# Diagonal blocks of a block-causal attention transposed from 64 partitions into 64 columns

## The chip, the cores and the metric

The kernel runs on one core of a Trainium2 chip. The metric is the device time of one execution in microseconds (us), the lower the better; the median of three executions of the kernel before is 1132.5 us (1131.85 to 1132.52).

## The reference, cut to what matters

Eight batches with eight heads each, 576 positions, head width 64. Attention is causal by blocks of 64 positions; its output, with the heads side by side (512 wide), goes through a low-rank mixing over positions (rank 32) and then a two-layer network (512 to 2048 to 512) with a residual.

```python
scores = scale * np.matmul(q, k.transpose(0, 1, 3, 2))
mask = block_i >= block_j                      # blocks of 64 positions
attn = np.exp(scores - np.max(scores, axis=-1, keepdims=True))
attn = attn / (np.sum(attn, axis=-1, keepdims=True) + 1e-09)
out = np.matmul(attn, v)
# x: out with the heads side by side
h = xt @ U @ V
u = x + h.transpose(0, 2, 1)
ch = np.maximum(u @ w_ch1, 0.0) @ w_ch2
return u + ch
```

## The kernel before, in words

**Order of the work.** Nothing is issued where it is written. Every step is a task of a planner (`Plan`): it has an engine, a cost in ns, a priority (the lower the earlier) and the tiles that it reads and writes. `Plan.issue` (L175) plays the tasks through with these costs and issues them in the order in which they would start. Each cost is shifted by up to 2% by a number that `VARIANT` (L61) sets, so another `VARIANT` gives another order. A task with `port=True`, and every task on GpSimd (POOL), takes a shared token, so that in the plan no VectorE (DVE) task of that kind runs beside one on POOL.

**Attention.** There are 64 heads. The 576 queries of a head are cut into five tiles: tile 0 holds queries 0 to 63, and tile i holds the 128 queries from 128 i - 64 on. Tile i has 128 i + 64 keys, so the tiles are 64, 192, 320, 448 and 576 keys wide. `softmax` (L1208) takes a group of tiles: TensorE (PE) writes the scores of the group into one PSUM bank, DVE takes the maximum of every row (L1255), ScalarE (ACT) takes the exponentials with their sums (L1266). An exponential waits for the maxima of all tiles of its group. Tile 4, the widest, has a PSUM tile of two banks (`bw`) of which there is one, and tile 1 stands beside it there; tiles 3 and 0 share a bank, tile 2 has its own. `normalise` takes the reciprocals on DVE (L1282, L1283) and multiplies the rows on POOL (L1292).

**Transposes.** `transpose` (L1304) turns the probabilities around, block by block of 128 keys, in four banks a head, with 15 transposes: a matmul with the block of probabilities as its weights and an identity matrix as the moving operand (L1325). Ten blocks have 128 queries that count. Five are the diagonal blocks, one for each tile, of which only 64 queries count. Before, these take 128 partitions and write 128 columns like the others: a permuted identity, `swap` (L1047), brings the 64 queries that count to the front, and the 64 columns behind them are written over by the next transposes, for which `moves` is sorted. ACT (L1302) and DVE (L1300 or L1344) copy the bank out, and `apply_v` (L1354) multiplies with V: heads 0 to 13 in float32 (L1368), the other 50 in two parts of reduced precision (L1384).

**What runs beside it.** From about 100 us on, the first part of the two-layer network runs in tasks of six float16 matmuls each with 288 moving columns (L661, L686) in two PSUM banks `bf`; their priority number is above that of all of attention, so they fill PE where attention has nothing ready. The rest of the network (`block_products`, L910) comes last. Weights are scaled to powers of two that `power` finds with two small matmuls (L418, weights of one column; L438, weights of one row), and `agree` (L491) makes two of these scales fit each other with eight tiny DVE instructions (L499 to L505).

Of the kernel before, what the change touches and what calls it, by code (L numbers as in the profile page):

```python
# [57 lines left out]
TAIL = {"PE": 165, "DVE": 78, "ACT": 105, "POOL": 20, "SP": 0}  # L58
INTO = {"PE": 355, "DVE": 60, "ACT": 60, "POOL": 200, "SP": 60}
NEAR, DL, PORT = 130, 3000, 200  # L60
VARIANT = 4  # L61
START = {"DVE": 5750, "ACT": 2750, "POOL": 3300, "SP": 700}
COL = 0.4555
LA, MP = 900.0, 500.0
# [214 lines left out]
def attention_then_mixer(  # L279
# [211 lines left out]
    def agree(prio):  # L491


        a, b, c, d = (scales[n] for n in range(4))

        def limits():
            t = joint.ap
            for x, y in ((0, 1), (1, 0)):
                nc.vector.scalar_tensor_tensor(out=t, in0=a[:, x : x + 1], scalar=0.125, in1=c[:, x : x + 1], op0=ALU.mult, op1=ALU.mult)  # L499
                nc.vector.scalar_tensor_tensor(out=t, in0=t, scalar=b[:, y : y + 1], in1=d[:, x : x + 1], op0=ALU.mult, op1=(ALU.min, ALU.max)[x])  # L500
                nc.vector.tensor_copy(d[:, x : x + 1], t)

        def ratio():
            nc.vector.scalar_tensor_tensor(out=joint.ap, in0=b[:, 0:1], scalar=2.0 ** -6, in1=d[:, 0:1], op0=ALU.mult, op1=ALU.mult)
            nc.vector.scalar_tensor_tensor(out=joint.ap, in0=joint.ap, scalar=a[:, 1:2], in1=c[:, 1:2], op0=ALU.mult, op1=ALU.mult)  # L505

        add("DVE", 1700, prio, limits, [a, b, c], [d, joint])
        add("DVE", 200, prio, ratio, [a, b, c, d], [joint])

    def level(w, bufs):  # L510

# [532 lines left out]
        factor[x] = buf(fp, [1, P], F32, f"factor{x}".replace(".", "_"))  # L1044
        nc.vector.memset(factor[x].ap, x)

    swap = buf(ap, [P, P], F32, "swap")  # L1047
    for a in (0, 64):
        nc.vector.tensor_copy(swap[:, a : a + 64], ident[:, 64 - a : P - a])
    warm = buf(ap, [P, 1], F32, "warm")  # L1050
    nc.vector.memset(warm.ap, 0.0)
    nc.scalar.activation(warm.ap, warm.ap, AF.Exp)
# [155 lines left out]
    def softmax(h, tiles, pr):  # L1208

        q1, k1, q2, k2, ss, mx = (r[h % len(r)] for r in (q1_r, k1_r, q2_r, k2_r, ss_r, mx_r))  # L1210
        raw = raw_r[h % len(raw_r)]
        wide = 4 in tiles
        bank = Buf(pool=banks_w if wide else banks_f if h < 8 and 3 in tiles else Rest(banks_a))

        parts, at = [], 0
        for i in tiles:
            parts.append((i, at))
            at += P * i + 64
        side = {1: (0, T), 0: (1, T), 2: (0, T)}

        def view(i, at):
            if i == 4:
                return bank[:, :, :T]
            rows, w = P if i else 64, P * i + 64
            return bank[:rows, side[i][0], side[i][1] : side[i][1] + w] if wide else bank[:rows, at : at + w]

        def products():
            for i, at in parts:
                qs = slice(P * i + 64 - (P if i else 64), P * i + 64)
                for j in range(2 if i == 4 else 1):  # L1230
                    o = bank[:, j, :T] if i == 4 else view(i, at)
                    ks = slice(j * T, j * T + T) if i == 4 else slice(0, P * i + 64)
                    if h < FS:
                        if not i:

                            o, qs = bank[:, 1, T : T + 64] if wide else bank[:, at : at + 64], slice(0, P)
                        nc.tensor.matmul(  # L1237
                            o, raw[:, qs], raw[:, S + ks.start : S + ks.stop], start=True, stop=True
                        )
                        continue  # L1240
                    nc.tensor.matmul(o, q1[:, qs], k1[:, ks], start=True, stop=False)
                    nc.tensor.matmul(o, q2[:, qs], k2[:, ks], start=False, stop=True)

        ns, ms = [], []
        for i in tiles:
            ns += [T] * 4 if i == 4 else [P * i + 64] * 2
            ms += [P if i else 64] * (4 if i == 4 else 2)
        if h < FS:
            add("PE", sum(1.667 * n for n in ns) / 2 + 60 * sum(i < 2 or i == 4 for i in tiles), pr, products, [raw], [bank])
        else:  # L1250
            add("PE", _pe(*ns, m=ms) + (60 if wide else 30 + 33 * sum(i < 2 for i in tiles)), pr, products, [q1, k1, q2, k2], [bank])
        for i, at in parts:
            add(
                "DVE", _dve(P * i + 64), pr,
                lambda i=i, at=at: nc.vector.tensor_reduce(  # L1255
                    out=mx[: P if i else 64, i : i + 1], in_=view(i, at), op=ALU.max, axis=AX.XY if i == 4 else AX.X,
                    negate=True,
                ),
                [bank], [mx.parts[i]],
            )  # L1260
        for i, at in parts:
            pt, rows = pt_r[i][h % PB[i]], P if i else 64

            def exponentials(i=i, at=at, pt=pt, rows=rows):
                out = pt[:rows, : P * i + 64]
                nc.scalar.activation(  # L1266
                    out.rearrange("p (j k) -> p j k", j=2) if i == 4 else out, view(i, at), AF.Exp,
                    bias=mx[:rows, i : i + 1], accum_out=ss[:rows, i, 0:1],
                )

            add(
                "ACT", _act(P * i + 64) + 188, pr, exponentials, [bank, *(mx.parts[i] for i in tiles)],
                [pt, ss.parts[i]],
            )

# [28 lines left out]
    def transpose(h, g, part, pr):  # L1304

        js = BLOCKS[g][part]
        bank, span = Buf(pool=banks_a), _span(g, js)
        n = span.stop - span.start


        moves = []
        for j in js:
            for i in range(5):
                q0 = max(P * i - 64, 0)
                a, b = max(q0, _first(g, j)), min(P * i + 64, QS[g + 1])
                if a < b:
                    c = _at(g, j).start - span.start + a - _first(g, j)
                    half = b - a < P
                    left = half and c + P > 512
                    moves.append((not half, i, j, swap if half and i and not left else ident, c - 64 if left else c))  # L1320
        moves.sort(key=lambda m: m[0])

        def products():
            for _, i, j, perm, a in moves:
                nc.tensor.transpose(  # L1325
                    out=bank[:, a : a + P], in_=pt_r[i][h % PB[i]][:, j * P : (j + 1) * P], identity=perm.ap
                )

        cost = 109 * len(moves)
        pts = [pt_r[i][h % PB[i]] for i in sorted({m[1] for m in moves})]  # L1330
        if h < FP:
            pw = pw_r[h % 2][g]
            b = pw.parts[part]
            add("PE", cost, pr, products, pts, [bank], hold=[b])
            copy((g, part) == (0, 1), n, pr, lambda: pw[:, span], lambda: bank[:, :n], [bank], [b])
            return
        ph, pl = ph_r[g], pl_r[g]
        bh, bl = ph.parts[part], pl.parts[part]
        add("PE", cost, pr, products, pts, [bank], hold=[bh, bl])
        copy(False, n, pr, lambda: ph[:, span], lambda: bank[:, :n], [bank], [bh])  # L1340
        m = n if js[-1] < 4 else n - 64
        low = slice(span.start, span.start + m)
        add(
            "DVE", _dve(m), pr, lambda: nc.vector.tensor_sub(pl[:, low], bank[:, :m], f32(ph[:, low])), [bank, bh], [bl]  # L1344
        )
        if m < n:

            end = _at(1, 4)
            add(
                "DVE", _dve(64) + 112, pr,  # L1350
                lambda: nc.vector.tensor_sub(ph[64:P, end], bank[0:64, m:n], f32(ph[0:64, end])), [bank, bh], [bh],
            )

    def apply_v(h, g, pr):  # L1354
# [6 lines left out]
        if h < FP:  # L1361
            vr, pt = vr_r[h // 2 % 2], pw_r[s][g]

            def whole_products():
                for j in range(NK[g]):

                    a, x = max(P * j - q0, 0), 5 * s + j
                    nc.tensor.matmul(  # L1368
                        bank[:, a:n], vr[:, x : x + 2, :], pt[:, _at(g, j)], start=(j == 0), stop=(j == NK[g] - 1)
                    )  # L1370

            cost = sum(5 + 1.667 * (n - max(P * j - q0, 0)) for j in range(NK[g]))
            add("PE", cost + 60, pr, whole_products, [vr, *pt.parts], [bank], hold=[xb])
            copy(False, n, pr, lambda: xt[me, q0:q1], lambda: bank[0:64, :n], [bank], [xb])
            return
        vs, tmp, ph, pl = vs_r[s], take(tmp_r, "tmp"), ph_r[g], pl_r[g]
# [107 lines left out]
    for h in range(NH):  # L1484
# [1 line left out]
        if h + 1 < NH:  # L1486
            split_qk(h + 1, max(pr - LA, 1.0))
        for g, tiles in ((1, (4, 3)), (0, (2, 1, 0))):
            for x in ((4, 1), (3, 0)) if g else ((2,),):
                softmax(h, x, pr + 10)  # L1490
            normalise(h, tiles, pr + 10)
        for g in (1, 0):
# [61 lines left out]
```

## Time and profile before

| | |
|---|---|
| median of 3 runs | 1132.5 us (1131.85 to 1132.52) |
| the profiled execution | 1132.52 us, its span 1130.7 us |
| PE busy | 1114.4 us, 99% of the span |
| DVE busy | 992.4 us, 88% |
| ACT busy | 809.8 us, 72% |
| POOL busy | 495.0 us, 44% |
| transposes of probabilities (L1325) | 960, of which 768 with `ident` and 192 with `swap` |

The profile is one execution. Matmuls overlap one another, and the end of a matmul is modelled, so the length of a single one says little; what one costs on PE is read from start to start. In a row of the timeline stand the start, the length from the first start to the last end, the engine and line, out<-in, the weights (rows\*columns), the moving operand (partitions x columns) and the count. `PE` is the matmul itself, `PEld` the load of its weights.

### The profile page before, as it was taken

Reading aid. Unit: us, or ns where it says so; the run is one execution under the profiler, and the core shown is the slowest. Engines: PE = TensorE matmul, PEld = TensorE weight load, DVE = VectorE, ACT = ScalarE, POOL = GpSimd, SP = SyncE. Lnnn points to the kernel's source line nnn. Section 1 sums busy time; section 2 is a strip of 40 time slices with the busy share of each in tenths; the row PEclk is TensorE's granted clock in tenths of the full one; section 3 lists DMA queues with packets and bytes.
Section 4 is the critical chain, followed back from the end, with each engine's and each line's share of the span. In section 5 each row is a group of like instructions: output and inputs, shape, how many; then the busy total and the mean of one; then the engine's idle time right before and its main releaser. Section 6 shows DMA issues by size and latency. Waiting matters only on the chain.

```text
span 1130.7 us, 25478 instructions
## 1 busy us (share of the span) xinstructions
PE 1114.4 (99%) x8952; PEld 929.1 (82%) x8952; DVE 992.4 (88%) x2247; ACT 809.8 (72%) x1994; POOL 495.0 (44%) x688
## 2 busy tenths in 40 slices
PE   9999999999999999999999999999999999999998
PEld 7787788888888888888888877777777777777776
DVE  6899899999889889899899765499999899998998
ACT  7878899999889889989998854254555555454543
POOL 5334558787787777787876676000000000000000
PEclk9999999999999999999999999999999999999999
DMA  4453656554563464545543141103122130404111
GB/s 127 129 148 117 181 153 173 145 158 128 145 164 104 137 176 129 149 149 138 148 122 88 55 148 58 59 22 105 54 74 76 52 116 12 127 12 116 33 53 43
DMA packets 76720, 122.14 MB, mean 108 GB/s; under 512 B 9008, under 2 KB 53040, under 8 KB 76592
## 3 DMA queue, kind: packets, MB, share of 16 engines
q1 hardware_dynamic: 76592, 120.51, 37.3%
q8 instruction: 71, 1.16, 0.4%
q14 instruction: 57, 0.47, 0.1%
HBM read 76.23 MB, written 29.49 MB: 94 GB/s over the span
## 4 chain that ended last, share of the span: by engine, by line
PE 67%; DVE 16%; ACT 10%; issue 3%; DMA 2%; POOL 1%; SPq 0%; ACTq 0%; DVEq 0%; POOLq 0%
PE bb L910 36%; PE bf L686 8%; PE bf L661 6%; PE ba L1325 5%; ACT p L1266 4%; DVE mx L1255 4%; DVE pl L1344 3%; PE ba L1384 3%; PE ba L1368 2%; ACT ph L1302 1%; DVE xt L1392 1%; PE bw L1237 1%; DMA raw<-in_qk_dram 1%; DVE hl L669 1%; DVE ut L1445 1%
## 5 line engine op out<-in xcount | busy, mean ns | idle before, releaser
L1292 POOL TENSOR_SCALAR p<-p,rv 128x576 f32<-128x576 f32 (+4 forms) x320 | 166.2, 533 | 88.1 <-DVE rv L1283 18.3
L910 PE MATMUL bb<-ph,w2l 128*128 128x288 f16 x560 | 151.0, 286 | 0.0
L910 PE MATMUL bb<-ph,w2h 128*128 128x288 f16 x560 | 151.0, 286 | 0.0
L910 PE MATMUL bb<-ph,w1h 128*128 128x288 f16 x560 | 148.7, 286 | 0.0
L910 PE MATMUL bb<-ph,w1l 128*128 128x288 f16 x560 | 148.7, 286 | 0.0
L832 ACT CAST ph<-hb 128x576 f16<-128x576 f32 x144 | 84.3, 590 | 82.8 <-PE bb L910 77.2
L910 PEld LDWEIGHTS <-w2h 128*128 128x128 f16 x1120 | 109.6, 98 | 27.5
L910 PEld LDWEIGHTS <-w1h 128*128 128x128 f16 x1120 | 109.6, 98 | 27.5
L1325 PE MATMUL ba<-ident,p 128*128 128x128 f32 x768 | 121.4, 275 | 2.7 <-POOL p L1292 1.5
L910 PE MATMUL bb<-pl,w2h 128*128 128x288 f16 x560 | 123.5, 286 | 0.0
L1344 DVE TENSOR_TENSOR pl<-ba,ph 128x512 fp32r<-128x512 f32 x200 | 105.8, 551 | 10.1 <-ACT ph L1302 7.1
L910 PE MATMUL bb<-pl,w1h 128*128 128x288 f16 x560 | 114.4, 286 | 0.0
L686 PE MATMUL bf<-hh,w2h 128*128 128x288 f16 x384 | 110.4, 287 | 0.2 <-DVE ot L698 0.2
L686 PE MATMUL bf<-hl,w2h 128*128 128x288 f16 x384 | 109.8, 286 | 0.0
L686 PE MATMUL bf<-hh,w2l 128*128 128x288 f16 x384 | 109.8, 286 | 0.0
L1325 PEld LDWEIGHTS ba<-ident,p 128*128 128x128 f32 x768 | 89.3, 141 | 9.4 <-issue 2.9
L1302 ACT CAST ph<-ba 128x512 fp32r<-128x512 f32 x200 | 92.0, 494 | 3.5 <-PE ba L1325 2.3
L834 DVE TENSOR_TENSOR pl<-hb,ph 128x576 f16<-128x576 f32 x144 | 91.4, 655 | 1.0
L686 PEld LDWEIGHTS <-w2h 128*128 128x128 f16 x768 | 75.1, 98 | 19.7 <-issue 1.1
L1266 ACT ACTIVATE p<-ba,mx 64x64 f32<-64x64 f32 (+1 forms) x176 | 86.0, 492 | 6.2 <-DVE mx L1255 5.4
L661 PEld LDWEIGHTS <-w1h 128*128 128x128 f16 x768 | 73.9, 98 | 18.7 <-issue 1.2
L1384 PE MATMUL ba<-ph,vs 128*128 128x256 f32 (+3 forms) x400 | 84.3, 269 | 0.5 <-DVE ut L1445 0.5
(191 smaller groups left out, 3105.4 us busy)
## 6 DMA issues: line engine op xcount, KB each, us to landing
raw<-in_qk_dram SPq DMA_DIRECT2D x63, 288.0 KB, 3.9
o_d<-ot SPq DMA_DIRECT2D x72, 144.0 KB, 1.8
vr<-in_v_dram SPq DMA_DIRECT2D x32, 320.0 KB, 3.6
ur<-u_d SPq DMA_DIRECT2D x64, 144.0 KB, 2.5
wr<-o_d SPq DMA_DIRECT2D x32, 288.0 KB, 3.1
out_dram<-wr SPq DMA_DIRECT2D x31, 288.0 KB, 2.3
st<-in_w_dram SPq DMA_DIRECT2D x16, 512.0 KB, 4.3
u_d<-ut SPq DMA_DIRECT2D x28, 288.0 KB, 2.5
```

The source lines that it names most:

```text
L661: nc.tensor.matmul(ps[:, :T], w()[wn][:, k, fs], m[k].ap, start=(i == 0), stop=(i == len(ops) - 1))
L686: nc.tensor.matmul(ps[:, :T], w()[wn][:, f, ms], hs[f][x].ap, start=(i == 0), stop=(i == len(ops) - 1))
L832: add("ACT", _act(n * T, True), E, lambda: nc.scalar.copy(h.ap[:, :n, :], x[0]()), [x[1]], [h])
L834: "DVE", _dve(n * T), E, lambda: nc.vector.tensor_sub(l.ap[:, :n, :], x[0](), h.ap[:, :n, :]), [x[1], h], [l],
L910: nc.tensor.matmul(bank[:, i, :T], x()[:, w(k)], p.ap[:, k, :], start=first and n == 0, stop=last and n == len(ops) - 1)
L1255: lambda i=i, at=at: nc.vector.tensor_reduce(out=mx[: P if i else 64, i : i + 1], in_=view(i, at), op=ALU.max, axis=AX.XY if i == 4 else AX.X,
L1266: nc.scalar.activation(out.rearrange("p (j k) -> p j k", j=2) if i == 4 else out, view(i, at), AF.Exp, bias=mx[:rows, i : i + 1], accum_ou ...
L1292: lambda x=x, rows=rows, i=i: nc.gpsimd.tensor_scalar(out=x, in0=x, scalar1=rv[:rows, i : i + 1], scalar2=1.0, op0=ALU.mult, op1=ALU.mult),
L1302: add("ACT", _act(n), pr, lambda: nc.scalar.copy(out(), inp()), reads, writes)
L1325: nc.tensor.transpose(out=bank[:, a : a + P], in_=pt_r[i][h % PB[i]][:, j * P : (j + 1) * P], identity=perm.ap)
L1344: "DVE", _dve(m), pr, lambda: nc.vector.tensor_sub(pl[:, low], bank[:, :m], f32(ph[:, low])), [bank, bh], [bl]
L1384: nc.tensor.matmul(bank[0 : c.stop, a:n], vs[:, j, c], x[:, _at(g, j)], start=(i == 0), stop=(i == len(ops) - 1))
```

## The change

Three things change in the work and some numbers in the planner.

1. A diagonal block is transposed from the 64 partitions that hold the queries that count (the first 64 for tile 0, the last 64 for the others), with the 64x64 corner of the identity as the moving operand, into 64 columns. `swap`, its two copies at the start and the sorting go; the moves of a bank stand in the order of keys and queries.
2. The groups of `softmax` are (4, 1, 0) and (3) in place of (4, 1) and (3, 0): tile 0 stands beside tiles 4 and 1 in the two-bank tile.
3. The tasks of `agree` take the token that keeps POOL away (`port=True`), with higher costs.
4. In the planner a 64-column transpose costs 55 instead of 109, the exponentials cost 6 more, the float32 product with V 30 more, and `VARIANT` is 210.

```diff
-VARIANT = 4
+VARIANT = 210
...
-        add("DVE", 1700, prio, limits, [a, b, c], [d, joint])
-        add("DVE", 200, prio, ratio, [a, b, c, d], [joint])
+        add("DVE", 2000, prio, limits, [a, b, c], [d, joint], port=True)
+        add("DVE", 450, prio, ratio, [a, b, c, d], [joint], port=True)
...
-    swap = buf(ap, [P, P], F32, "swap")
-    for a in (0, 64):
-        nc.vector.tensor_copy(swap[:, a : a + 64], ident[:, 64 - a : P - a])
...
-                "ACT", _act(P * i + 64) + 188, pr, exponentials, [bank, *(mx.parts[i] for i in tiles)],
+                "ACT", _act(P * i + 64) + 194, pr, exponentials, [bank, *(mx.parts[i] for i in tiles)],
...
                 if a < b:
-                    c = _at(g, j).start - span.start + a - _first(g, j)
-                    half = b - a < P
-                    left = half and c + P > 512
-                    moves.append((not half, i, j, swap if half and i and not left else ident, c - 64 if left else c))
-        moves.sort(key=lambda m: m[0])
+                    moves.append((i, j, _at(g, j).start - span.start + a - _first(g, j), b - a))
 
         def products():
-            for _, i, j, perm, a in moves:
+            for i, j, c, w in moves:
+                qs = slice(P - w, P) if i else slice(0, w)
                 nc.tensor.transpose(
-                    out=bank[:, a : a + P], in_=pt_r[i][h % PB[i]][:, j * P : (j + 1) * P], identity=perm.ap
+                    out=bank[:, c : c + w], in_=pt_r[i][h % PB[i]][qs, j * P : (j + 1) * P], identity=ident[qs, qs]
                 )
 
-        cost = 109 * len(moves)
+        cost = sum(109 if w == P else 55 for *_, w in moves)
...
-            add("PE", cost + 60, pr, whole_products, [vr, *pt.parts], [bank], hold=[xb])
+            add("PE", cost + 90, pr, whole_products, [vr, *pt.parts], [bank], hold=[xb])
...
-            for x in ((4, 1), (3, 0)) if g else ((2,),):
+            for x in ((4, 1, 0), (3,)) if g else ((2,),):
```

In the planned order of PE (engine queue, from its start; the names are out<-in, `ba` and `bf` PSUM banks, `p_0_n` the probabilities of a tile of head 0; the size is that of the output) the four banks of head 0 stand like this before:

```order
L1325 MATMUL ba_98<-swap,p_0_174 128x128
L1325 MATMUL ba_98<-ident,p_0_176 128x128
L1325 MATMUL ba_98<-ident,p_0_174 128x128
L1325 MATMUL ba_98<-ident,p_0_176 128x128 x2
L1325 MATMUL ba_95<-swap,p_0_170 128x128
L1325 MATMUL ba_95<-swap,p_0_172 128x128
L1325 MATMUL ba_95<-ident,p_0_172 128x128
L1325 MATMUL ba_96<-ident,p_0_168 128x128
L1325 MATMUL ba_96<-ident,p_0_170 128x128
L1325 MATMUL ba_96<-ident,p_0_172 128x128
```

and after, at the same place (L1320 is the same line of code):

```order
L1320 MATMUL ba_98<-ident,p_0_171 128x128
L1320 MATMUL ba_98<-ident,p_0_173 128x128
L1320 MATMUL ba_98<-ident,p_0_171 128x64
L1320 MATMUL ba_98<-ident,p_0_173 128x128
L1320 MATMUL ba_98<-ident,p_0_173 128x64
L1235 MATMUL bf_90<-raw_161 128x448
L1320 MATMUL ba_95<-ident,p_0_165 128x64
L1320 MATMUL ba_95<-ident,p_0_167 128x128
L1320 MATMUL ba_95<-ident,p_0_169 128x128
L1320 MATMUL ba_96<-ident,p_0_167 128x64
L1320 MATMUL ba_96<-ident,p_0_169 128x128
L1320 MATMUL ba_96<-ident,p_0_169 128x64
```

All ten rows before read 128 partitions; after, five of the eleven transposes read 64 partitions, and they alternate with those that read 128. Over the whole program 320 of the 960 transposes become ones of 64 partitions, and the order of PE changes 602 times between such a transpose and a matmul of another kind (301 times in, 301 times out).

The exponentials of head 0 on ACT before (`bw` is the two-bank tile, the names again out<-in):

```order
L1266 ACTIVATE p_0_176,ss_166<-bw,mx_189 128x576
L1266 ACTIVATE p_0_170,ss_166<-bw,mx_189 128x192
L1266 ACTIVATE p_0_174,ss_166<-bf_90,mx_189 128x448
L1266 ACTIVATE p_0_168,ss_166<-bf_90,mx_189 64x64
L1266 ACTIVATE p_0_172,ss_166<-ba_95,mx_189 128x320
```

and after:

```order
L1264 ACTIVATE p_0_173,ss_163<-bw,mx_186 128x576
L1264 ACTIVATE p_0_167,ss_163<-bw,mx_186 128x192
L1264 ACTIVATE p_0_165,ss_163<-bw,mx_186 64x64
L1264 ACTIVATE p_0_171,ss_163<-bf_90,mx_186 128x448
L1264 ACTIVATE p_0_169,ss_163<-ba_95,mx_186 128x320
```

The 64x64 tile has moved from the bank of tile 3 to the two-bank tile; the number of instructions is the same.

More of the change, by code (lines that the diff above doesn't have):

```diff
@@ L500, in limits @@
                 nc.vector.scalar_tensor_tensor(out=t, in0=t, scalar=b[:, y : y + 1], in1=d[:, x : x + 1], op0=ALU.mult, op1=(ALU.min, ALU.max)[x])
-                nc.vector.tensor_copy(d[:, x : x + 1], t)
+                last = nc.vector.tensor_copy(d[:, x : x + 1], t)
+            return last
         def ratio():
             nc.vector.scalar_tensor_tensor(out=joint.ap, in0=b[:, 0:1], scalar=2.0 ** -6, in1=d[:, 0:1], op0=ALU.mult, op1=ALU.mult)
-            nc.vector.scalar_tensor_tensor(out=joint.ap, in0=joint.ap, scalar=a[:, 1:2], in1=c[:, 1:2], op0=ALU.mult, op1=ALU.mult)
-        add("DVE", 1700, prio, limits, [a, b, c], [d, joint])
-        add("DVE", 200, prio, ratio, [a, b, c, d], [joint])
+            return nc.vector.scalar_tensor_tensor(out=joint.ap, in0=joint.ap, scalar=a[:, 1:2], in1=c[:, 1:2], op0=ALU.mult, op1=ALU.mult)
+        add("DVE", 2000, prio, limits, [a, b, c], [d, joint], port=True)
+        add("DVE", 450, prio, ratio, [a, b, c, d], [joint], port=True)
     def level(w, bufs):
@@ L1316, in transpose @@
                 if a < b:
-                    c = _at(g, j).start - span.start + a - _first(g, j)
-                    half = b - a < P
-                    left = half and c + P > 512
-                    moves.append((not half, i, j, swap if half and i and not left else ident, c - 64 if left else c))
-        moves.sort(key=lambda m: m[0])
+                    moves.append((i, j, _at(g, j).start - span.start + a - _first(g, j), b - a))
         def products():
-            for _, i, j, perm, a in moves:
+            for i, j, c, w in moves:
+                qs = slice(P - w, P) if i else slice(0, w)
                 nc.tensor.transpose(
-                    out=bank[:, a : a + P], in_=pt_r[i][h % PB[i]][:, j * P : (j + 1) * P], identity=perm.ap
+                    out=bank[:, c : c + w], in_=pt_r[i][h % PB[i]][qs, j * P : (j + 1) * P], identity=ident[qs, qs]
                 )
-        cost = 109 * len(moves)
-        pts = [pt_r[i][h % PB[i]] for i in sorted({m[1] for m in moves})]
+        cost = sum(109 if w == P else 55 for *_, w in moves)
+        pts = [pt_r[i][h % PB[i]] for i in sorted({m[0] for m in moves})]
         if h < FP:
```

## The prediction

> **What bounds the kernel now.** I read the page's totals first, then the busy time by stage, then the chain of work that ended last.
>
> ```profile
> span 1130.7 us, 25478 instructions
> ...
> PE 1114.4 (99%) x8952; PEld 929.1 (82%) x8952; DVE 992.4 (88%) x2247; ACT 809.8 (72%) x1994; POOL 495.0 (44%) x688
> ...
> PE 67%; DVE 16%; ACT 10%; issue 3%; DMA 2%; POOL 1%; SPq 0%; ACTq 0%; DVEq 0%; POOLq 0%
> ```
>
> PE is busy for 99% of the span, and two thirds of the chain run through it. The execution took 1132.52 us, 1.8 us more than its span, and it is the slowest of the three runs shown, 0.02 us above their median; so the sum below is made against 1132.5. Busy alone proves little, since matmuls overlap; the stages say more.
>
> ```profile
> core 0: us, PE busy (x) PEld busy (x) DVE busy (x) ACT busy (x) POOL busy (x), PEclk, DMA share, GB/s
> 0.00:100.00 100.00, 95.35 (x562) 78.96 (x563) 83.30 (x256) 78.87 (x226) 45.24 (x90) 1.00 0.47 133
> 133.00:141.00 8.00, 6.87 (x48) 5.94 (x46) 7.79 (x17) 6.34 (x15) 5.59 (x5) 1.00 0.85 221
> 200.00:600.00 400.00, 394.80 (x3336) 345.06 (x3334) 359.39 (x972) 364.04 (x1022) 314.49 (x440) 1.00 0.51 142
> 730.00:1130.00 400.00, 397.32 (x3244) 317.12 (x3241) 370.79 (x591) 200.51 (x339) 0.00 (x0) 1.00 0.21 63
> ```
>
> The clock is granted in full throughout (1.00). From 730 us on PE is a closed stream: 3244 matmuls in 400 us are 0.123 us each, and the rows of float16 matmuls below start 0.12 us apart. From 200 to 600 us attention and the first part of the network share PE, which stands idle for 5 us of 400, while DVE and ACT are at 90% and 91%. There is still network work left when attention is over:
>
> ```profile
> L686 PE MATMUL bf<-hh,w2h 128*128 128x288 f16 x102 | 29.2, 286 | 0.0
> ```
>
> This row (from the groups between 640 and 730 us) is one of six of its kind, 102 matmuls each of three and 96 each of three others. So a PE slot that attention gives back before 640 us can be filled with one of these 594 matmuls, and the end comes earlier by the same time. I take the sum of PE's work as what sets the end.
>
> **The transposes.** What one costs now, and what stands around it:
>
> ```profile
> 236.19 0.29 PE L686 MATMUL bf<-hl,w2h 128*128 128x288 f16 x1
> 236.32 0.60 PE L1325 MATMUL ba<-ident,p 128*128 128x128 f32 x4
> 236.75 0.27 PE L1325 MATMUL ba<-swap,p 128*128 128x128 f32 x1
> 236.86 0.93 PE L1325 MATMUL ba<-ident,p 128*128 128x128 f32 x7
> ```
>
> Four take 0.60 us with the last one 0.27 long, so they start (0.60 - 0.27)/3 = 0.11 us apart, and so does the one with `swap` (236.75 to 236.86). Is that the load of 128 columns of weights or the stream of 128 moving columns? Two places tell them apart. Half as many columns of weights:
>
> ```profile
> 369.64 0.29 PE L686 MATMUL bf<-hl,w2h 128*128 128x288 f16 x1
> 369.76 0.27 PE L1410 MATMUL ba<-ident,xt 128*64 128x128 f32 x1
> 369.87 0.29 PE L686 MATMUL bf<-hh,w2h 128*128 128x288 f16 x1
> ```
>
> A transpose with 64 columns of weights and 128 moving columns still holds PE for 0.11 us. And a transpose behind a short matmul:
>
> ```profile
> 606.99 0.40 PE L1425 MATMUL ba<-xl,ust 128*64 128x128 f32 x4
> 607.23 0.40 PE L1325 MATMUL ba<-ident,p 128*128 128x128 f32 x2
> ```
>
> The four of L1425 start (607.23 - 606.99)/4 = 0.06 us apart, and the transpose with its 128 columns of weights comes on at the same step: its load fits into 0.06 us. So the stream is the bound, at 0.109 us for 128 columns (0.60, 0.93 and 0.27 give 0.109 to 0.110). Float32 matmuls with other widths agree:
>
> ```profile
> 101.18 2.01 PE L1368 MATMUL ba<-spare,vr 128*128 128x256 f32 x10
> ```
>
> By L1368 these are six with 256 columns, two with 192 and two with 64; the first nine stream 1984 columns in 2.01 - 0.27 = 1.74 us, 0.88 ns a column, against 0.109/128 = 0.85 ns. A 64-column stream is then 0.055 us, just under the 0.06 that the load needs. I take 0.059 for a diagonal block, a saving of **0.050 us** each; the ends are 0.109 (the load counts after all: nothing saved) and 0.028 (if PE could step as for 64 columns of reduced precision, which I do not use since the load stands in its way).
>
> The Trainium skill speaks against the change here: "TensorE: Matmul & The Clock Gate", section on LDWEIGHTS, gives a load as the number of its columns over 1.2, 107 ns for 128, whatever the rows. By that alone the transposes would be bound by their loads and the sum would be zero; the trace differs, with 0.06 us.
>
> There are 320 diagonal blocks, five in each of 64 heads. The products with V (durations in ns, then first and last start in us) tell where the heads lie:
>
> ```profile
> L1368 PE MATMUL ba<-spare,vr x224: 219/352/537, 15.2 to 136.4; 128*128 128x256 f32 x42, 128*128 128x192 f32 x28, 128*128 128x64 f32 x28, 128*128 128x320 f32 x14
> L1384 PE MATMUL ba<-ph,vs x400: 191/267/416, 150.9 to 639.9; 128*128 128x256 f32 x51, 128*128 128x192 f32 x34, 128*128 128x64 f32 x33, 128*128 128x320 f32 x16
> ```
>
> Heads 14 to 63 take 489 us, some 10 us each, and run where the network fills PE: 250 x 0.050 = **12.5 us**. Heads 0 to 13 end at 136.4 us; before that PE is idle more (4.65 us of the first 100) and little else is ready; I count half of 70 x 0.050, **1.75 us** (ends 0 and 3.5).
>
> **The other edits.** `swap`'s copies are the first thing to go:
>
> ```profile
> 1.33 1.17 DVE L1049 COPY swap<-ident 128x64 f32<-128x64 f32 x2
> ...
> 6.90 1.02 DVE L1255 TENSOR_REDUCE mx<-bw 128x1 f32<-128x576 f32 x2 [3.05 <-PE bw L1237]
> ```
>
> DVE waits 3.05 us for the first scores afterwards, so this is worth nothing. Tile 0 beside tiles 4 and 1:
>
> ```profile
> L1255 DVE TENSOR_REDUCE mx<-ba 64x1 f32<-64x64 f32 x56 | 11.4, 204 | 0.2
> ...
> L1266 ACT ACTIVATE p<-ba,mx 64x64 f32<-64x64 f32 x56 | 17.4, 311 | 0.2
> ```
>
> The same instructions run; the exponentials of tile 4 wait for one more maximum (0.20 us), and the two-bank tile is held 0.20 + 0.31 us longer in a head of 10 us, while the bank of tile 3 comes free that much sooner. PE has network work under either wait: zero, and if that cover were gone, up to 0.2 us x 64 heads = 13 us against it at worst. `agree`:
>
> ```profile
> 133.68 0.54 DVE L499 SCALAR_TENSOR_TENSOR joint<-sc 128x1 f32<-128x1 f32 x1
> 134.26 0.79 DVE L500 SCALAR_TENSOR_TENSOR joint<-joint,sc 128x1 f32<-128x1 f32 x1
> ...
> 135.27 1.14 DVE L499 SCALAR_TENSOR_TENSOR joint<-sc 128x1 f32<-128x1 f32 x1
> 136.45 1.34 DVE L500 SCALAR_TENSOR_TENSOR joint<-joint,sc 128x1 f32<-128x1 f32 x1
> ...
> 138.82 0.15 DVE L504 SCALAR_TENSOR_TENSOR joint<-sc 128x1 f32<-128x1 f32 x1
> ```
>
> The four long ones take 3.81 us where one of that kind can take 0.15, so without POOL beside them up to 3.2 us go from DVE. Queued behind them are the maxima of the next head, and PE loses 8.00 - 6.87 = 1.13 us in this stretch. In return POOL's queue stands still for the planned 2000 + 450 ns. I count -0.5 us, with ends of -1.1 and +2.5. The new costs and `VARIANT` make the planner deal the same instructions in another order; no row prices that. The three runs lie 0.7 us apart, which is no measure of it; as an estimate I allow 4 us both ways, three quarters of PE's 5.2 idle us between 200 and 600.
>
> Sum: 12.5 + 1.75 + 0.5 = 14.75, and 1132.5 - 14.75 = **1118 us**. Own range of this case: 3.5 more or less for the first heads and `agree`, 4 for the order: 1111 to 1125.
>
> **The rivals.** *PE empties itself at every change of rows (slower).* There are places in the trace where PE stops between two matmuls that use different parts of its array:
>
> ```profile
> 500.86 0.29 PE L686 MATMUL bf<-hh,w2l 128*128 128x288 f16 x1
> 500.98 0.29 PE L686 MATMUL bf<-hl,w2h 128*128 128x288 f16 x1
> 501.20 0.38 PE L418 MATMUL ba<-ident,oneu 128*1 128x128 f32 x2
> 501.51 0.30 PE L686 MATMUL bf<-hh,w2h 128*128 128x288 f16 x1
> ...
> 260.00 0.38 PE L418 MATMUL ba<-ident,oneu 128*1 128x128 f32 x2
> 260.31 0.44 PE L1325 MATMUL ba<-ident,p 128*128 128x128 f32 x2
> ```
>
> Into L418 (weights of one column) the step is 0.22 instead of 0.12 us; its two matmuls step by 0.11, so they end at 501.42 and 260.22, and the next starts 0.09 later. A transpose behind it also shows its load (two take 0.44, not 0.38): 0.15 in all. If 64 rows beside 128 are such a change, it comes 602 times: 602 x 0.095 = 57 us, and 0.055 of load at the 301 changes into a diagonal block and at the 200 that lead to another transpose, 28 us. Less 16 saved that is 1132.5 + 69 = **1201 us** (without the loads 1173). It decides from 0.027 us a change on (16/602). Against it: weights of 64 columns beside 128 show no stop at all (369.76 to 369.87 and 607.23 above). No row here has 64 rows. The Trainium skill, "TensorEngine Tiling (Array Packing)", Key Properties, says that changing the tiling mode drains TensorE; the trace agrees for one column, and not for 64 columns. I give it 0.20.
>
> *The load is not hidden.* If the load is the floor (0.11 us whatever the moving columns), or a load for 64 rows can't run under a matmul of 128, each diagonal block gives back what it saved: 1132.5 us; if it is laid bare on the way out too, 602 x 0.055 - 16 = 17 us more, **1132 to 1150**. For it: the load behind L418 is shown in full. Against it: 607.23. 0.06.
>
> *Attention is paced by DVE and ACT.* At 90% and 91% they may be what the heads wait for; then PE's freed slots help only as far as the network's own steps on DVE and ACT find room, and I count a quarter of the gain: **1129 us**. Against it: PE idles 5 us in 400. 0.06.
>
> **How the numbers follow.** Forecast 0.68, the stops 0.20, the load 0.06, DVE and ACT 0.06. The likeliest is the first: 1118 us. The range leaves out the stops alone, on top of a tenth of the first case on its low side: 1109 to 1150. A measurement can tell some 0.2% (2.3 us) from no change. Faster: 0.68 + 0.05; within 0.2%: 0.02 of the load and 0.01 of DVE and ACT, with 0.01 for a bad order; slower: 0.20 + 0.03.
>
> **What would show it.** Right: 320 transposes of 64 rows that start about 0.06 us apart from what follows; first part of the network done some 13 us earlier, the last stage as long as before. Wrong: 0.2 us and more from a 128-row transpose to a 64-row one, and a weight load that starts about 0.09 us behind the end of the stream. PE's idle time between 200 and 600 us well over 5 us would mean that other engines pace the heads.

## The result and the profile after

The changed kernel takes **1180.89 us** (median of 4 runs, 1180.61 to 1181.47), the kernel before beside it 1132.51 us (4 runs): a ratio of 1.0427, with a 95% interval of 1.0409 to 1.0445. It is slower by 48.4 us, where 1118 was forecast and 1150 was the upper end of the range. The first rival, stops at changes of rows, comes nearest, with 1201 us (1173 without its loads).

From the page of the kernel after: the span, the totals of the engines and the shares of the chain that ended last.

```profile
span 1179.7 us, 25430 instructions
...
PE 1169.6 (99%) x8952; PEld 933.7 (79%) x8952; DVE 994.2 (84%) x2245; ACT 825.3 (70%) x1994; POOL 494.8 (42%) x688
...
PE 94%; ACT 3%; DVE 1%; DMA 1%; issue 1%; POOL 0%; SPq 0%; ACTq 0%
```

PE has the same 8952 matmuls and is busy for 55.2 us more (1169.6 against 1114.4); the record of a matmul lasts some 0.27 us, so a stop that is shorter counts as busy. Its idle time falls from 1130.7 - 1114.4 = 16.3 us to 10.1, so the span grows by 49.0. The chain, two thirds PE before, is now PE nearly alone; DVE's 16% and ACT's 10% in it have gone to 1% and 3%.

Busy time by stage of the kernel after; the last row is the last stage, taken from 780 us on, where 730 was taken before.

```profile
core 0: us, PE busy (x) PEld busy (x) DVE busy (x) ACT busy (x) POOL busy (x), PEclk, DMA share, GB/s
0.00:100.00 100.00, 96.77 (x518) 73.62 (x519) 72.67 (x225) 75.10 (x210) 43.26 (x84) 1.00 0.41 119
133.00:141.00 8.00, 8.00 (x65) 6.68 (x64) 6.28 (x18) 7.64 (x22) 4.95 (x10) 1.00 0.56 136
200.00:600.00 400.00, 399.32 (x3102) 322.97 (x3100) 335.78 (x896) 342.18 (x934) 289.65 (x406) 1.00 0.48 133
780.00:1180.00 400.00, 396.28 (x3235) 316.23 (x3233) 369.60 (x589) 199.89 (x338) 0.00 (x0) 1.00 0.22 63
```

From 200 to 600 us PE is busy for 399.32 us and does 3102 matmuls, where it did 3336 with 5 us idle. Each now takes more of PE's time, at a clock that is still granted in full; DVE, ACT and POOL all do less in the same stretch, so they wait for PE. The last stage is what it was (3235 matmuls in 400 us, before 3244).

The weight loads of one bank in the kernel after (timeline in several narrow windows, starting just before the sixth of six 128-row transposes; start and length in us):

```profile
527.00 0.15 PEld L1320 LDWEIGHTS ba<-ident,p 128*128 128x128 f32 x1
527.30 0.14 PEld L1320 LDWEIGHTS ba<-ident,p 64*128 64x128 f32 x1 [0.16 <-issue]
527.51 0.14 PEld L1320 LDWEIGHTS ba<-ident,p 128*128 128x128 f32 x1
527.77 0.14 PEld L1320 LDWEIGHTS ba<-ident,p 64*128 64x128 f32 x1
527.97 0.10 PEld L687 LDWEIGHTS <-w2h 128*128 128x128 f16 x1
```

And the matmuls that belong to the first four of these loads, at the end of one row of nine:

```profile
526.44 0.29 PE L687 MATMUL bf<-hl,w2h 128*128 128x288 f16 x1
526.56 1.48 PE L1320 MATMUL ba<-ident,p 128*128 128x128 f32 x9
527.97 0.30 PE L687 MATMUL bf<-hh,w2h 128*128 128x288 f16 x1
```

The row of nine is six 128-row transposes, then 64, 128 and 64 rows. At 0.109 us each the sixth starts at 526.56 + 5 x 0.109 = 527.10 and its stream ends at 527.21. The load of the first 64-row one starts only at 527.30: PE stands for **0.09 us**, and nothing is waited for that the profile names ("issue"). From the 64-row one to the next it is 0.21 us: its load, no longer hidden (0.055), its stream (0.055) and a second stop. The 128-row one between takes 0.26: its load laid bare, 0.109, and again a stop. The three take 527.97 - 527.21 = 0.76 us where three 128-row transposes took 0.33, so each diagonal block costs 0.22 us more than it did. Many such blocks show in the groups by shape of the kernel after, where loads of 64 rows have 19.1 us of "issue" ahead of them, which is not named at its loads of 128 rows:

```profile
L1320 PEld LDWEIGHTS ba<-ident,p 128*128 128x128 f32 x640 | 75.1, 141 | 17.2 <-POOL p L1290 1.6 <-ACT p L1264 0.2 <-POOL z L379 0.2
L1320 PEld LDWEIGHTS ba<-ident,p 64*128 64x128 f32 x320 | 40.8, 135 | 45.3 <-issue 19.1 <-POOL p L1290 1.5 <-DVE pl L1339 1.2
```

Where in the program the time came in, by the first and last products with V and of the network's first part, after:

```profile
L1379 PE MATMUL ba<-ph,vs x400: 191/266/415, 155.9 to 700.4; 128*128 128x256 f32 x51, 128*128 128x192 f32 x34, 128*128 128x64 f32 x33, 128*128 128x320 f32 x16
L687 PE MATMUL bf<-hh,w2h x384: 282/286/301, 136.5 to 773.7; 128*128 128x288 f16 x192
```

and of the network's first part before (the products with V stand in the prediction):

```profile
L686 PE MATMUL bf<-hh,w2h x384: 283/286/302, 122.4 to 722.5; 128*128 128x288 f16 x192
```

The first 14 heads are 5.0 us later (150.9 to 155.9), the other 50 take 544.5 us in place of 489.0, and 9 us come back after attention: 73.3 us of network are left then, before 82.6, since more of it was done beside attention. The last stage begins some 51 us late.

### The profile page after: what moved, and what is told of

Same layout as the page of the kernel before. It is cut to its first block, busy times and chain, and to the rows that moved or that the text cites. A ratio compares the mean times of both kernels' runs of the same rounds, so it can differ in the third digit from the quotient of the medians.

```text
span 1179.7 us, 25430 instructions
## 1 busy us (share of the span) xinstructions
PE 1169.6 (99%) x8952; PEld 933.7 (79%) x8952; DVE 994.2 (84%) x2245; ACT 825.3 (70%) x1994; POOL 494.8 (42%) x688
## 4 chain that ended last, share of the span: by engine, by line
PE 94%; ACT 3%; DVE 1%; DMA 1%; issue 1%; POOL 0%; SPq 0%; ACTq 0%
PE bb L911 35%; PE ba L1320 13%; PE bf L687 12%; PE bf L662 11%; PE ba L1379 6%; PE ba L1363 3%; PE bw L1239 2%; PE bw L1235 2%; PE bw L1240 2%; PE ba L1405 1%; PE ba L1420 1%; PE ba L1239 1%; PE ba L1240 1%; PE ba L1235 1%; ACT p L1264 1%; PE ba L1435 1%
## 5 line engine op out<-in xcount | busy, mean ns | idle before, releaser
L1320 PE MATMUL ba<-ident,p 128*128 128x128 f32 (+1 forms) x960 | 182.1, 284 | 1.3 <-POOL p L1290 1.3
L1320 PEld LDWEIGHTS ba<-ident,p 128*128 128x128 f32 (+1 forms) x960 | 115.9, 139 | 62.5 <-issue 19.4
L1300 ACT CAST ph<-ba 128x512 fp32r<-128x512 f32 x200 | 95.4, 492 | 27.1 <-PE ba L1320 23.7
L1264 ACT ACTIVATE p<-bw,mx 128x576 f32<-128x576 f32 (+2 forms) x192 | 92.9, 488 | 4.9 <-DVE mx L1253 3.9
L1253 DVE TENSOR_REDUCE mx<-bw 128x1 f32<-128x576 f32 (+2 forms) x192 | 77.8, 431 | 9.3 <-PE bw L1235 7.7
```

The costliest lines, as they stand in the source:

```text
L1253: lambda i=i, at=at: nc.vector.tensor_reduce(out=mx[: P if i else 64, i : i + 1], in_=view(i, at), op=ALU.max, axis=AX.XY if i == 4 else AX.X,
L1264: nc.scalar.activation(out.rearrange("p (j k) -> p j k", j=2) if i == 4 else out, view(i, at), AF.Exp, bias=mx[:rows, i : i + 1], accum_ou ...
L1300: add("ACT", _act(n), pr, lambda: nc.scalar.copy(out(), inp()), reads, writes)
L1320: nc.tensor.transpose(out=bank[:, c : c + w], in_=pt_r[i][h % PB[i]][qs, j * P : (j + 1) * P], identity=ident[qs, qs])
```

## The experiments

The theories: **stops** (PE empties at each change between 64 and 128 rows, the first rival); **load** (a load for 64 rows is not hidden, and no more); **order** (it is the planner's new order, or another of the edits, and not the transposes). The eight kernels ran on two chips, four on each; the kernel before took 1132.16 us (13 runs) and 1132.23 us (7 runs) there.

**One part alone, and the rest alone.** The kernel before with nothing but the 64-row transposes and their cost in the planner (in part; `swap` and the sorting go as in the change):

```diff
 # to the kernel before
...
+                qs = slice(P - w, P) if i else slice(0, w)
-                    out=bank[:, a : a + P], in_=pt_r[i][h % PB[i]][:, j * P : (j + 1) * P], identity=perm.ap
+                    out=bank[:, c : c + w], in_=pt_r[i][h % PB[i]][qs, j * P : (j + 1) * P], identity=ident[qs, qs]
...
-        cost = 109 * len(moves)
+        cost = sum(109 if w == P else 55 for *_, w in moves)
```

> The kernel before with the 64-row transposes alone; grouping, agree, planner numbers and VARIANT stay as before. Theory A (PE empties itself at each of some 600 changes between 64-row and 128-row matmuls, 0.09 us and an uncovered load): the whole slowdown is here, 1175 to 1200 us, and a 128-row transpose ahead of a 64-row one takes about 0.20 us instead of 0.11. Theory B (the other edits, above all tile 0 beside the widest tile, and the new order cost the time): 1118 to 1136 us.

Measured: 1189.59 us, ratio 1.0509 (1.0493 to 1.0524).

The changed kernel with the transposes of before (`swap`, 128 rows, the sorting), so with the grouping, `agree`, the other costs and `VARIANT` 210 (in part):

```diff
 # to the kernel after
...
-                qs = slice(P - w, P) if i else slice(0, w)
-                    out=bank[:, c : c + w], in_=pt_r[i][h % PB[i]][qs, j * P : (j + 1) * P], identity=ident[qs, qs]
+                    out=bank[:, a : a + P], in_=pt_r[i][h % PB[i]][:, j * P : (j + 1) * P], identity=perm.ap
```

> The changed kernel with the transposes of before (128 rows, 128 columns, the permuted identity); all its other edits stay. Theory A: 1132 us give or take 5, since the other edits move no PE work. Theory B: 1175 us or more.

Measured: 1132.81 us, ratio 1.0007 (0.9998 to 1.0017, 10 runs). The chains of the two, 64-row transposes alone first:

```profile
PE 90%; DVE 5%; ACT 3%; issue 1%; DMA 1%; SPq 0%; POOL 0%; ACTq 0%; DVEq 0%
```

```profile
PE 73%; DVE 12%; ACT 11%; issue 3%; POOL 1%; DMA 0%; SPq 0%; ACTq 0%; POOLq 0%
```

The transposes alone bring all of the loss, and the move of the chain to PE with it; on the kernel before the rest is neutral. Order falls as the cause. Together the two do not simply add up: beside the 64-row transposes the rest saves 8.7 us (1189.59 against 1180.89). From 700 to 800 us PE is idle for 5.6 us with the transposes alone and for none in the changed kernel; which of the other edits does that, no run shows.

**64 columns without 64 rows.** Each diagonal transpose is replaced by a float16 matmul of zeros with 128 rows and 64 moving columns, in the changed kernel and in the one with the 64-row transposes alone (the edit in part). The diagonal blocks are left out of the result by this.

```diff
+    blank = buf(ap, [P, P], F16, "blank")
+    nc.vector.memset(blank.ap, 0.0)
...
+                if w < P:
+                    nc.tensor.matmul(bank[:, c : c + w], blank.ap, blank[:, 0:w], start=True, stop=True)
+                    continue
```

> The changed kernel with the same float16 matmuls of zeros in place of the diagonal transposes (the diagonal blocks are left out of the product with V). Theory A: about 1113 us, as with the rest of before, 65 us below the changed kernel. Theory B: not below 1160 us, since tile 0 still stands beside the widest tile.

Measured: 1117.33 us (1115.12 to 1119.04), ratio 0.9868 (0.9854 to 0.9883).

> As the 64-row transposes alone, but in place of each diagonal transpose stands a float16 matmul of zeros with 128 rows and 64 moving columns into the same place; the diagonal blocks of the probabilities are left out of the product with V. The work per diagonal block falls from 0.109 to about 0.05 us on PE and no change of rows is left. Theory A, and the sum of PE's work sets the end: 320 x 0.06 = 19 us less than before, about 1113 us. If DVE and ACT pace the heads instead: 1126 us or more. Theory B has nothing to say of it.

Measured: 1126.93 us, ratio 0.9954 (0.9937 to 0.9971). That is not the 1113 us of the theory that PE's sum sets the end, but what was expected if DVE and ACT pace the heads.

The matmuls of a bank in the first of the two (timeline of PE):

```profile
285.56 0.20 PE L1323 MATMUL ba<-blank 128*128 128x64 f16 x1
285.60 0.31 PE L1325 MATMUL ba<-ident,p 128*128 128x128 f32 x1
285.74 0.19 PE L1323 MATMUL ba<-blank 128*128 128x64 f16 x1
285.77 0.41 PE L662 MATMUL bf<-uh,w1l 128*128 128x288 f16 x2
```

With 128 rows there is no stop on either side: 0.03 us to the next matmul (285.74 to 285.77). The transpose behind the first one takes 0.14 us in place of 0.109, as part of its load shows. The three take 285.77 - 285.56 = 0.21 us where three 128-column transposes took 0.33, so a block costs some 0.06 us less, 19 us for 320 of them (an estimate from this bank), and 14.8 us come through (1132.16 - 1117.33). So a saving on PE's path is worth most of its size in this kernel, as the forecast had assumed; that it is the rows that spoil it, the next run shows. With the order and the other edits of before, the same cut brought only 5.2 us. In that kernel PE is idle for 6.9 us in one stretch of a hundred, and the granted clock is 0.98 there:

```profile
600.00:700.00 100.00, 93.09 (x760) 74.15 (x759) 69.91 (x151) 64.64 (x135) 57.85 (x63) 0.98 0.27 84
```

The kernel before has 0.95 us of idle time and a clock of 1.00 in the same stretch, the end of attention. The longest waits of PE there are for steps of the network itself, 2.8 us for ACT (L644) and 2.8 us for DVE (L669). So a cut on PE is worth its size only where the network's own steps keep up.

**64 rows without float32 and without transposing.** The same matmul of zeros, now from 64 rows (the diagonal blocks are left out again):

```diff
 # to the kernel with the float16 matmuls and all other edits
-                    nc.tensor.matmul(bank[:, c : c + w], blank.ap, blank[:, 0:w], start=True, stop=True)
+                    nc.tensor.matmul(bank[:, c : c + w], blank[qs, :], blank[qs, 0:w], start=True, stop=True)
```

> The changed kernel with float16 matmuls of zeros in place of the diagonal transposes, as in the run at 1117 us, but with 64 rows in place of 128 (the diagonal blocks are left out of the product with V). If any change of rows stops PE: 602 x 0.09 us more, 1165 to 1180 us. If only transposes, or only float32, do: 1112 to 1122 us.

Measured: 1160.00 us, ratio 1.0247 (1.0232 to 1.0262), a little below the 1165 to 1180 expected if any change of rows stops PE. A bank of it, on the timelines of PE and of its loads:

```profile
284.84 0.27 PE L1410 MATMUL ba<-ident,xt 128*128 128x128 f32 x1
285.04 0.09 PEld L1323 LDWEIGHTS <-blank 64*128 64x128 f16 x1 [0.17 <-issue]
285.05 0.20 PE L1323 MATMUL ba<-blank 64*128 64x64 f16 x1
285.18 0.33 PE L1325 MATMUL ba<-ident,p 128*128 128x128 f32 x1
285.44 0.20 PE L1323 MATMUL ba<-blank 64*128 64x64 f16 x1
285.57 0.30 PE L687 MATMUL bf<-hh,w2h 128*128 128x288 f16 x1
```

Rows are the only difference to the kernel of 1117.33 us, and they cost 42.7 us, 0.071 for each of 602 changes (less than a stop: from the one kernel to the other PE's waits fall from some 42 us to 23, by the estimate explained with the rival's size below). The transpose of L1410 streams until 284.84 + 0.109 = 284.95, and the load of the 64-row matmul starts 0.09 us later. The step out of a 64-row matmul is 0.13 us where it was 0.03, so PE stops for 0.09 to 0.10 us on that side too; the 128-row transpose takes 0.26, with its float32 load laid bare. Neither the number format nor the transposing makes the stop. Load alone falls with this: the load itself starts late, and with float16 the loss stays.

**Fewer changes.** The 64-row transposes of a bank first, so that some stand side by side: 384 changes of rows in place of 602.

```diff
 # to the kernel after, ahead of products()
+        moves.sort(key=lambda m: m[3])
```

> The changed kernel with the 64-row transposes of a bank put ahead of its 128-row ones: the same 960 transposes, but 384 changes of rows in place of 602. If the cost hangs on the changes (0.09 us each over some 1125 us without any): about 1160 us, and two 64-row transposes in a row start some 0.06 us apart. If a 64-row transpose is slow by itself, wherever it stands: 1180 us as before, and 0.2 us between the two.

Measured: 1152.25 us, ratio 1.0179 (1.0162 to 1.0196), where about 1160 was expected if the cost hangs on the changes. Two 64-row loads on the same rows side by side in it, and the 128-row one behind them (timeline in several narrow windows; the second row counts the second load and the third together, the last row is the third alone):

```profile
438.53 0.13 PEld L1322 LDWEIGHTS ba<-ident,p 64*128 64x128 f32 x1 [0.17 <-ACT p L1264]
...
438.58 0.34 PEld L1322 LDWEIGHTS ba<-ident,p 64*128 64x128 f32 x2
438.79 0.14 PEld L1322 LDWEIGHTS ba<-ident,p 128*128 128x128 f32 x1
```

The same 960 transposes with 218 changes fewer are 28.6 us faster, 0.131 us a change, which lies between a stop alone (0.09) and a stop with a bare load (0.15). In between the two 64-row loads, some 0.055 us apart, there is no stop; behind the second there is one (0.34 - 0.14 = 0.20 us from load to load). As matmuls the two start 0.11 us apart (so do most of the 128 such pairs), the bare load of the first and its stream, and not 0.20; so a 64-row transpose is not slow by itself.

**Which rows.** All 64-row transposes read partitions 0 to 63 in place of 64 to 127 for tiles 1 to 4; their diagonal blocks are left out of the result by this.

```diff
 # to the kernel after
-                qs = slice(P - w, P) if i else slice(0, w)
+                qs = slice(0, w)
```

> The changed kernel with every 64-row transpose taken from partitions 0 to 63 in place of 64 to 127 (for tiles 1 to 4 the masked rows, so their diagonal blocks are left out). If the number of rows makes the stop: 1176 to 1186 us. If it is the start at partition 64: most stops go, 1125 to 1140 us.

Measured: 1182.31 us, ratio 1.0443 (1.0427 to 1.0458). It does not matter whether the 64 rows are the first or the last.

**The order alone.** The kernel before with `VARIANT` 210:

```diff
-VARIANT = 4
+VARIANT = 210
```

> The kernel before with VARIANT = 210 alone: the same instructions in another order. It measures what an order is worth: 1128 to 1137 us if my allowance of 4 us holds; more than that would put part of the 48 us on the order.

Measured: 1139.44 us (1137.79 to 1141.42), ratio 1.0066 (1.0051 to 1.0081). The same instructions dealt in another order cost 7.2 us, while with the other edits this number makes nothing slower (1.0007 above). A part of it goes with the clock: three of the four executions were granted 0.997 or 0.998 of it, and the one at 1.000 took 1137.79 us, 5.6 more than before.

None of these versions that computes the whole result is faster than the kernel before. A transpose from 128 rows into 64 columns, for which the float16 matmuls of 128 rows stand, was not tried.

## Why the prediction was wrong

- **PE's sum sets the end**: right for the changed kernel, where 55.2 us more of busy PE and 6.2 us less idle are the 49.0 of the span. For a saving it depends on the order: without 64 rows a cut of some 19 us brought 14.8 with the new order and the other edits, and 5.2 without them.
- **A 64-column stream takes 0.055 to 0.059 us**: right, where nothing changes around it (438.53 to 438.58). The saving of 0.050 a block would be there, but every 64-row block in these runs has a change of rows beside it.
- **The load fits into 0.06 us and stays hidden**: right between matmuls of equal rows, and wrong at a change, where 0.055 us lie bare on the way in and on the way out to another transpose (0.26 us is 0.055 and 0.109 and a stop of 0.09).
- **The step that failed**: the sum put the stops at nothing. They were a rival with a chance of 0.20, and the argument against them was that weights of 64 columns show no stop. Measured were 0.09 us at each of 602 changes and bare loads of 0.055 us besides; with the saving set against them PE's steps are some 67 us longer (worked out below), where they were to be 14.25 us shorter. The argument read the wrong rows: weights of 64 columns keep the 128 rows, and so do those of L418, which have one column and stop PE all the same. The kernel before has a nearer row that the prediction did not read, the matmuls of L438 with weights of one row:

```profile
108.03 0.60 PE L1325 MATMUL ba<-ident,p 128*128 128x128 f32 x4
108.56 0.38 PE L438 MATMUL bf<-roww,factor 1*128 1x2 f32 x2
108.87 0.42 PE L661 MATMUL bf<-uh,w1l 128*128 128x288 f16 x2
```

  The four transposes stream until 108.03 + 4 x 0.109 = 108.47, and L438 starts 0.09 us later: the stop stood in the trace at a change of rows. The Trainium skill, "TensorEngine Tiling (Array Packing)", Key Properties, says that changing the tiling mode drains TensorE; for 64 rows the trace agrees, with 0.09 us at a change, and for 64 columns it does not. A stop seen in this trace decided from 0.027 us on, and it was three times that: the rival should have been the forecast.
- **The rival's size**: +69 us forecast, +48.4 measured. Its terms held on PE: at 0.22 us a block 320 blocks are 70 us. What it left out are the waits that PE had before. An estimate of them sets every step from one matmul's start to the next, in both traces, against the short ones among the steps between matmuls of the same shapes (the 15% quantile over all ten traces; from 5% to 50% the fall is the same 18 us). By it the steps without waits add up to some 67 us more after than before, and the waits fall from some 40 us to 22; 67 - 18 is the 49 of the span. In the first 14 heads the steps grow by 11 us and the waits fall by 6, which are the 5.0 of delay, where a share of 14/64 in the 69 is 15. Most of these waits are shorter than the record of a matmul, so the totals of the page show only 6.2 us of them as idle time.
- **The other edits at zero and `agree` at -0.5**: right in sum (ratio 1.0007: +0.8 us, interval -0.2 to +1.9). The four long instructions of `agree`, 3.81 us before, now take 0.74, as these rows of DVE after show. The 3.1 us of DVE were worth nothing that can be seen:

```profile
154.45 0.14 DVE L499 SCALAR_TENSOR_TENSOR joint<-sc 128x1 f32<-128x1 f32 x1
154.63 0.22 DVE L500 SCALAR_TENSOR_TENSOR joint<-joint,sc 128x1 f32<-128x1 f32 x1
...
155.07 0.16 DVE L499 SCALAR_TENSOR_TENSOR joint<-sc 128x1 f32<-128x1 f32 x1
155.26 0.22 DVE L500 SCALAR_TENSOR_TENSOR joint<-joint,sc 128x1 f32<-128x1 f32 x1
```

- **The order, 4 us both ways**: too narrow. `VARIANT` alone moved the time by 7.2 us, 5.6 at the full clock. What makes 210 fit the changed kernel and not the one before stays open.
- **DVE and ACT pace the heads**: not in the changed kernel, where they lost their places in the chain as PE had more to do, and not much with its order when PE had less to do (14.8 of 19 us came through). With the order of before it was otherwise: 5.2 us, near the quarter that this rival counts, with PE waiting for the network's own steps.

## What to carry to other kernels

Before a matmul is cut from 128 rows to 64, count the changes between the two that it makes among its neighbours, and set the saving against 0.09 us for each of them and a bare float32 load besides. Here 16 us of saving stood against 602 changes. A straight line through the two kernels measured, 48.4 us lost at 602 changes and 20.0 at 384, meets no loss at some 230 changes, fewer than four for each of 64 heads; this is an estimate, well outside what was run. If a trace shows a stop of the same kind anywhere (here L438), take that row as the price, and not the absence of one at a place that changes something else.

## What the hardware showed beyond that

Two 64-row transposes that read different rows (0 to 63 and 64 to 127) and stand side by side start together. In the kernel after, a row of weight loads:

```profile
290.79 0.14 PEld L1320 LDWEIGHTS ba<-ident,p 64*128 64x128 f32 x2
291.00 0.14 PEld L1320 LDWEIGHTS ba<-ident,p 128*128 128x128 f32 x1
```

Both loads fit into 0.14 us, the length of one, where two on the same rows started some 0.055 us apart. The next start, 0.21 us behind them, is that of a single one: the second block takes no time of its own, and the stop is paid once for both. In 19 places of that kernel two 64-row transposes stand side by side; in 16 of them the matmuls start 3 to 5 ns apart, in the others 0.11 us. With every 64-row transpose on partitions 0 to 63 all 19 are some 0.11 us apart, so it is the different rows that let them run together.

Not every number of rows below 128 makes PE stop. In the kernel before, the matmuls of L1440 have weights of 96 rows:

```profile
295.79 0.41 PE L661 MATMUL bf<-uh,w1l 128*128 128x288 f16 x2
295.94 0.52 PE L1440 MATMUL ba<-v,t 96*128 96x288 f32 x2
296.30 0.37 PE L1384 MATMUL ba<-ph,vs 128*128 128x256 f32 x2
```

The second matmul of L661 starts at 295.79 + 0.41 - 0.29 = 295.91. From there it takes 0.39 us to L1384, for three matmuls of 288 moving columns, 0.13 each, where those of the network alone start 0.12 us apart. That leaves no room for a stop of 0.09 us on the way into 96 rows or out of them, whereas 64 rows and the one row of L438 show it.
